# Where the output projections of a cached attention block stand from unit 24 on

## The chip, the cores and the metric

The kernel runs on one core of one Trainium2 chip. The metric is device time in microseconds, the median of five runs. The engines are called as the profile calls them: PE (TensorE matmuls) and PEld (its weight loads), DVE (VectorE), ACT (ScalarE), POOL (GpSimd) and SP (SyncE, which here only issues DMAs).

## The reference

Eight batches of 112 query rows attend to a cache of 512 keys in 32 heads of width 192, with a query projection in front and an output projection behind, all in bf16:

```
B, Sq, D = 8, 112, 640
H, Sk, Dh = 32, 512, 192
q = (x @ wq).reshape(B, Sq, H, Dh).transpose(0, 2, 1, 3)
scores = einsum("bhqd,bhkd->bhqk", q, k_cache) * Dh ** -0.5
p = softmax(scores)
o = einsum("bhqk,bhkd->bhqd", p, v_cache)
out = o.transpose(0, 2, 1, 3).reshape(B, Sq, H * Dh) @ wo
```

## The kernel before

The 32 heads are cut into NG = 8 groups of four. A unit is one batch in one group: NU = 64 units, unit u being group u // 8 and batch u % 8. A unit needs its own K and its own V (four loads of 192 KB each).

**PE's order** is written out in `on_tensor`. Iteration i, from 1 to 63, issues:

1. `do_S(i)` (L954): scores of unit i, 96 small matmuls. The scores fill PSUM banks 0 to 3, which exist once, so `do_S(i)` waits until ACT has taken the exponentials of unit i-1 out (semaphore `aEX`).
2. `do_T(i-2)` (L983): six transposes of the normalised result of unit i-2.
3. `do_pair(i, 0)`: the projection work of slot 0.
4. `do_PV(i-1)` (L972): probabilities times V, 16 matmuls. It waits on `aT` until ACT's copy `tevac(i-2)` (L1069) has taken the transposes of step 2 out, since the two share PSUM banks.
5. `do_pair(i, 1)`: the projection work of slot 1.

Iterations 64 and 65 finish what is left: `do_PV(63)`, two `do_T`, and three projections.

**Projection work** comes in pairs (two PSUM banks, 6 and 7, one for each half h). `("Q", g, c)` is a sixth of the query projection of group g: five steps of two 448-column matmuls. `("O", g, m)` is the output projection of 128 of the 896 output rows for the four heads of group g: six steps of two 320-column matmuls; its result is added into `acc` (or, for the last group, written to `ob`) by DVE in `do_OE` (L1134). A Q pair is taken out by ACT (`evac`, L1036). The first matmul of a step loads the weights (L933), the second keeps them (L858). There are seven O pairs for each group and six Q pairs for each group but the first.

The table `slot[i, j]` says which pair stands in slot j of iteration i. A pair stands there whole (FULL), or its first steps in one slot (FRONT) and the rest in a later one (BACK). `pairs` is the order that results; `bank_free` makes each pair wait until the pair before it in that order has been taken out of the banks.

**DVE's order** in iteration i: two transposes of K (`do_KT`, L1111), the sums of an O pair that ended in slot 0, a third K transpose, reciprocal and scaling of unit i-1 (`do_NM`, L1117 and L1120, after `do_PV(i-1)`), the sums of an O pair that ended in slot 1, a fourth K transpose. From iteration 22 on, the transposes done by the end of iteration i reach the first quarter of unit i+3.

**ACT's order** in iteration i: first exponential of unit i, `tevac(i-2)`, second exponential, Q pair of slot 0, third and fourth exponential, half of the scaling of unit i-1 (`norm`, L1059), Q pair of slot 1. `tevac` of a unit overwrites columns of `oT` that the O pairs of the group before must have read, so it waits on `pO`.

**SP's order** is a list in rounds: in round u, K of unit u, V of unit u-1, then at most one of the five `wq` loads of a later group, then at most one third of the `wo` of a group (two loads of 160 KB). K has three raw buffers, V four, `wo` two; a load waits for its buffer to be free, and everything behind it in the list waits too. The `wo` load of group g waits for the last O pair of group g-2.

Of the kernel before, what the change touches and what calls it, by code (L numbers as in the profile page):

```python
# [666 lines left out]
def build_main(nc, x, k_cache, v_cache, wq, wo, out, flag, regs, hints):  # L667
# [3 lines left out]
    NG = H // 4  # L671
    NU = NG * B
    DC = D // 128
    R = B * SQ
    MT = R // 128
# [9 lines left out]
    FULL, FRONT, BACK = range(3)  # L685
# [12 lines left out]
    slot = {(i, j): None for i in range(NU + 2) for j in range(2)}  # L698

    def put(i, j, pair, part=FULL):  # L700
        assert slot[i, j] is None
        slot[i, j] = (pair, part)

    def halves(i, j, pair):
        put(i, j, pair, FRONT)
        put(i + j, 1 - j, pair, BACK)

    for g in range(NG):
        i0 = 8 * g
        if g > 0 and g < NG - 1:  # L710
            put(i0, 0, ("O", g - 1, 4))
            put(i0, 1, ("Q", g + 1, 0))
            put(i0 + 1, 0, ("O", g - 1, 5))
            halves(i0 + 1, 1, ("Q", g + 1, 1))
            put(i0 + 2, 1, ("O", g - 1, 6))
            put(i0 + 3, 0, ("Q", g + 1, 2))
            halves(i0 + 3, 1, ("Q", g + 1, 3))
            put(i0 + 4, 1, ("O", g, 0))
            put(i0 + 5, 0, ("Q", g + 1, 4))
            halves(i0 + 5, 1, ("Q", g + 1, 5))  # L720
            put(i0 + 6, 1, ("O", g, 1))
            put(i0 + 7, 0, ("O", g, 2))
            put(i0 + 7, 1, ("O", g, 3))
        elif g == 0:
            put(1, 0, ("Q", 1, 0))
            put(1, 1, ("Q", 1, 1))
            put(2, 0, ("Q", 1, 2))
            halves(2, 1, ("Q", 1, 3))
            put(3, 1, ("Q", 1, 4))
            put(4, 0, ("O", 0, 0))  # L730
            halves(4, 1, ("Q", 1, 5))
            put(5, 1, ("O", 0, 1))
            put(6, 0, ("O", 0, 2))
            put(7, 1, ("O", 0, 3))
        else:
            halves(i0, 0, ("O", g - 1, 4))
            halves(i0 + 1, 0, ("O", g - 1, 5))
            put(i0 + 2, 0, ("O", g - 1, 6), FRONT)
            put(i0 + 3, 0, ("O", g - 1, 6), BACK)
            for m in range(4):  # L740
                halves(i0 + 4 + m, 0, ("O", g, m))
            put(i0 + 8, 0, ("O", g, 4))
            put(i0 + 9, 0, ("O", g, 5))
            put(i0 + 9, 1, ("O", g, 6))
    pairs = [slot[i, j][0] for i in range(NU + 2) for j in range(2) if slot[i, j] and slot[i, j][1] != BACK]
    done_at = [slot[i, j][0] for i in range(NU + 2) for j in range(2) if slot[i, j] and slot[i, j][1] != FRONT]
    before = {p: pairs[n - 1] if n else ("Q", 0, 5) for n, p in enumerate(pairs)}
# [3 lines left out]
    assert pairs == done_at and len(pairs) == 6 * (NG - 1) + MT * NG  # L751
    assert [p for p in pairs if p[0] == "Q"] == [("Q", g, c) for g in range(1, NG) for c in range(6)]
    assert [p for p in pairs if p[0] == "O"] == [("O", g, m) for g in range(NG) for m in range(MT)]

    kt_ahead, done = [], 4
    for i in range(NU + 2):
# [4 lines left out]
    with ExitStack() as es:  # L761
# [58 lines left out]
        def W(eng, s, v):  # L820
            if v > 0:
                eng.wait_ge(s, v)

        def bank_of(pair, h):
            return (3, 5)[h] if pair == aside else 6 + h

        def bank_free(eng, pair, h):
            if pair == aside:
                return
            k, g, c = before[pair]  # L830
            if k == "Q":
                W(eng, aQ, q_index[g, c, h] + 1 if g else 11 + h)
            else:
                W(eng, vO, o_index[g, c, h] + 1)
# [4 lines left out]
        def last_unit(m):  # L839
            return -(-128 * (m + 1) // SQ) - 1  # L840
# [6 lines left out]
        def on_tensor(pe):  # L847
# [53 lines left out]
            def do_pair(i, j):  # L901
                if slot[i, j] is None:
                    return
                (k, g, c), part = slot[i, j]
                pair = (k, g, c)
                if k == "Q":
                    if c == 0:
                        W(pe, gW, DC * g)
                    n, width, inc = DC, HQ, pQ
                else:  # L910
                    if part != BACK and 8 * g + last_unit(c) + 1 > min(i - 2 + j, NU - 2):
                        W(pe, aT, 8 * g + last_unit(c) + 1)
                    n, width, inc = 6, HO, pO
                steps = {FULL: range(n), FRONT: range(n // 2), BACK: range(n // 2, n)}[part]
                fill = FILL.get((i, j), 1)
                apart = (i, j) == (NU + 1, 1)
                for q, hs in [(q, [h]) for h in range(2) for q in steps] if apart else [(q, range(2)) for q in steps]:
                    if k == "Q":
                        w = wqs[:, g % 2, q, 128 * c:128 * (c + 1)]
                        rhs = [xT[:, q, HQ * h:HQ * (h + 1)] for h in range(2)]  # L920
                    else:
                        if c == 0 and q % 2 == 0:
                            W(pe, mWO[g % 2][q // 2], 32 * (g // 2 + 1))
                        w = oT[:, q, 128 * c:128 * (c + 1)]
                        rhs = [wos[:, g % 2, q, HL * h:HL + (D - HL) * h] if apart else wos[:, g % 2, q, HO * h:HO * (h + 1)]
                               for h in range(2)]
                    for h in hs:
                        if q == 0:
                            bank_free(pe, pair, h)
                        cuts = fill if q else 1  # L930
                        for f in range(cuts):
                            cs = slice(0, (HL, D - HL)[h]) if apart else slice(width * f // cuts, width * (f + 1) // cuts)
                            mm = (pe.matmul if h == hs[0] and f == 0 else held)(ps[:, bank_of(pair, h), cs], w, rhs[h][:, cs], q == 0,  # L933
                                                                               q == n - 1 and f == cuts - 1)
                        if q == n - 1:
                            mm.then_inc(inc, 1)
# [305 lines left out]
        def on_sync(sp):  # L1242
# [10 lines left out]
            def load_wq(g, dc):  # L1253
                src = wq[128 * dc:128 * (dc + 1), 4 * DH * g:4 * DH * (g + 1)]
                if g == 0:
                    add(wqs[:, 0, dc, :], src, mW0[dc], 16, [])
                else:
                    add(wqr[:, dc, :], src, mWQ[dc], 16 * g, [(gW, DC * (g - 2) + dc + 1)])

            def load_wo(g, k):  # L1260
                r0 = 4 * DH * g + 256 * k
                src = wo[r0:r0 + 256].rearrange("(p e) d -> p e d", e=2)
                for e in range(2):
                    add(wos[:, g % 2, 2 * k + e, :], src[:, e], mWO[g % 2][k], 32 * (g // 2 + 1),
                        [(pO, 2 * MT * (g - 1))])

            def load_k(u):
                g, b = divmod(u, B)
                src = k_cache[b, 4 * g:4 * g + 4].rearrange("a (j s) d -> (a j) (s d)", s=16)
                for h in range(KP[u]):  # L1270
                    cs = slice(16 // KP[u] * DH * h, 16 // KP[u] * DH * (h + 1))
                    add(kr[u % NK][:].rearrange("p s d -> p (s d)")[:, cs], src[:, cs], mK[u % NK], 16 * sum(KP[u % NK:u + 1:NK]),
                        [(vKT, 4 * (u - NK + 1))])

            def load_v(u):
                g, b = divmod(u, B)
                for a in range(4):
                    add(vs[u % NV][:, a, 32:32 + 4 * DH], v_cache[b, 4 * g + a].rearrange("(m t) d -> m (t d)", t=4),
                        mV[u % NV], 64 * (u // NV + 1), [(pPV, u - NV + 1)])
# [16 lines left out]
            for u in range(4, NU + 1):  # L1296
                if u < NU:
                    load_k(u)
                if u - 1 >= 3:
                    load_v(u - 1)  # L1300
                for g in range(2, NG):
                    d = u - max(4, 8 * (g - 1) - 6)
                    if 0 <= d < DC:
                        load_wq(g, d)
                for g in range(1, NG):
                    d = u - (8 * g - 1)
                    if 0 <= d < 3:
                        load_wo(g, d)
            for n, (dst, src, s, count, waits) in enumerate(loads):
# [13 lines left out]
        for part, eng in ((on_tensor, nc.tensor), (on_scalar, nc.scalar), (on_vector, nc.vector), (on_gpsimd, nc.gpsimd), (on_sync, nc.sync)):  # L1323
            part(eng)
# [50 lines left out]
```

## Time and profile before

| | |
|---|---|
| median of five runs | 394.38 us (392.94 to 395.18) |
| the profiled execution's own time | 393.64 us |
| its span on the core | 391.8 us |
| PE busy | 385.5 us (98% of the span) |
| PEld, DVE, ACT, POOL busy | 242.9, 283.4, 250.8, 153.0 us |
| granted TensorE clock | 1.0 |
| moved by DMA | 120.00 MB, mean 306 GB/s |
| chain that ended last | PE 96% |

A time of the profiled execution is compared with its own 393.64 us; the 1.8 us between that and the span lie around the program. A matmul's record is about twice as long as the distance to the next start (the records of neighbours overlap), so distances between starts tell how fast PE goes, and the busy column does not.

### The profile page before, as it was taken

The numbers are of one execution on the slowest core, as the hardware profiler recorded it, in microseconds if no ns is written. First come the engines' busy times: TensorE is split into PE (matmuls) and PEld (weight loads), VectorE is DVE, ScalarE is ACT, GpSimd is POOL, SyncE is SP. The second block draws the span as 40 slices with busy tenths as digits, with TensorE's granted clock in tenths as the row PEclk, the third lists the DMA queues.
The fourth block names the chain that finished last, engine by engine and source line by source line (L and its number), as shares of the span: only waits on it lengthen the run. The fifth ranks groups of instructions, "written<-read, shape, count | busy, mean of one in ns | idle before, by whom it ended". The sixth has DMA issues, their size and how long they took to land.

```text
span 391.8 us, 19832 instructions
## 1 busy us (share of the span) xinstructions
PE 385.5 (98%) x8833; PEld 242.9 (62%) x8286; DVE 283.4 (72%) x506; ACT 250.8 (64%) x550; POOL 153.0 (39%) x352
## 2 busy tenths in 40 slices
PE   8999989999999999999999999999999999999997
PEld 3556665656656665665665665665666665667764
DVE  1665787676786887776787866876768766789935
ACT  3767765766656765657746677557675667657662
POOL 5442543334443354333451354432553332333331
PEclk9999999999999999999999999999999999999999
DMA  8999999999999999999999899989999789999912
GB/s 263 375 371 341 333 321 349 338 303 360 357 360 305 337 301 365 316 310 320 314 337 311 279 310 340 327 286 300 301 341 301 232 298 296 313 318 295 305 53 70
DMA packets 88584, 120.00 MB, mean 306 GB/s; under 512 B 9776, under 2 KB 88496, under 8 KB 88496
## 3 DMA queue, kind: packets, MB, share of 16 engines
q1 hardware_dynamic: 88496, 118.72, 91.4%
q8 instruction: 68, 1.11, 1.2%
q14 instruction: 20, 0.16, 0.1%
HBM read 117.54 MB, written 1.15 MB: 303 GB/s over the span
## 4 chain that ended last, share of the span: by engine, by line
PE 96%; issue 1%; DMA 1%; POOL 1%; DVE 0%; ACT 0%; SPq 0%
PE ps L933 22%; PE ps L972 22%; PE ps L858 21%; PE ps L954 21%; PE ps L983 6%; PE ps L892 2%; DMA xs<-in_x_dram 1%; PE ps L877 1%; PE ps L854 1%; POOL vm L1214 0%; DMA vs<-in_v_cache_dram 0%; PE ps L897 0%; POOL wqs L1207 0%; DVE kt L1111 0%; DVE acc L1131 0%
## 5 line engine op out<-in xcount | busy, mean ns | idle before, releaser
L1111 DVE STREAM_TRANSPOSE kt<-kr 128x384 int32<-128x384 int32 x256 | 195.1, 869 | 11.5 <-DMA kr<-in_k_cache_dram 11.3
L1052 ACT ACTIVATE pT<-ps 128x448 bf16<-128x448 f32 x256 | 130.8, 559 | 84.5 <-PE ps L954 83.6
L954 PEld LDWEIGHTS ps<-qT,kt 32*128 32x128 bf16 x6144 | 77.2, 93 | 30.2 <-issue 22.4
L933 PE MATMUL ps<-wos,oT 128*128 128x320 bf16 (+2 forms) x342 | 93.2, 299 | 0.6 <-issue 0.6
L972 PE MATMUL ps<-vm,pT 128*128 128x193 bf16 x768 | 91.5, 247 | 1.0 <-ACT oT L1069 0.8
L858 PE MATMUL ps<-wos,oT 128*128 128x320 bf16 x330 | 91.2, 299 | 0.0
L954 PE MATMUL ps<-qT,kt 32*128 32x112 bf16 x6144 | 87.8, 208 | 0.6 <-issue 0.4
L1214 POOL COPY vm<-vs 128x1152 int32<-128x1152 int32 x64 | 73.5, 1148 | 32.7 <-issue 25.8
L1231 POOL TENSOR_SCALAR bad<-rinv 112x4 f32<-112x4 f32 x64 | 14.6, 229 | 180.8 <-DVE rinv L1117 180.6
L972 PEld LDWEIGHTS ps<-vm,pT 128*128 128x128 bf16 x768 | 67.9, 97 | 22.1 <-ACT oT L1069 11.6
L933 PE MATMUL ps<-xT,wqs 128*128 128x448 bf16 x210 | 74.0, 352 | 0.3 <-POOL wqs L1207 0.3
L858 PE MATMUL ps<-xT,wqs 128*128 128x448 bf16 x210 | 73.9, 352 | 0.0
L1059 ACT ACTIVATE os<-ps,rinv 112x192 bf16<-112x192 f32 x128 | 48.0, 436 | 27.4 <-DVE rinv L1117 27.4
L972 PE MATMUL ps<-vs,pT 128*128 128x193 bf16 x256 | 62.6, 245 | 0.0
L933 PEld LDWEIGHTS ps<-wos,oT 128*128 128x128 bf16 x342 | 33.2, 97 | 43.7 <-issue 35.8
L1036 ACT ACTIVATE qT<-ps 128x448 bf16<-128x448 f32 x96 | 47.7, 552 | 18.7 <-PE ps L933 13.8
L1134 DVE TENSOR_TENSOR acc<-ps,acc 128x320 f32<-128x320 f32 x84 | 37.3, 485 | 27.6 <-PE ps L933 27.6
L1069 ACT ACTIVATE oT<-ps 128x672 bf16<-128x672 bf16 x64 | 46.4, 725 | 2.1 <-PE ps L983 2.1
L1117 DVE RECIPROCAL rinv<-ps 112x4 f32<-112x4 f32 x64 | 11.1, 173 | 48.0 <-PE ps L972 48.0
L933 PEld LDWEIGHTS ps<-xT,wqs 128*128 128x128 bf16 x210 | 20.4, 97 | 34.5 <-issue 28.9
L1120 DVE TENSOR_TENSOR os<-ps,rinv 112x384 bf16<-112x384 f32 x64 | 35.7, 558 | 7.3 <-DVE rinv L1117 0.5
L1207 POOL COPY wqs<-wqr 128x384 bf16<-128x384 bf16 x70 | 33.3, 510 | 5.0 <-DMA wqr<-in_wq_dram 5.0
(44 smaller groups left out, 154.6 us busy)
## 6 DMA issues: line engine op xcount, KB each, us to landing
kr<-in_k_cache_dram SPq DMA_DIRECT2D x256, 192.0 KB, 4.1
vs<-in_v_cache_dram SPq DMA_DIRECT2D x256, 192.0 KB, 4.0
wos<-in_wo_dram SPq DMA_DIRECT2D x48, 160.0 KB, 4.3
wqr<-in_wq_dram SPq DMA_DIRECT2D x35, 192.0 KB, 5.1
wqs<-in_wq_dram SPq DMA_DIRECT2D x5, 192.0 KB, 4.5
out_dram<-xs SPq DMA_DIRECT2D x6, 160.0 KB, 1.8
xs<-in_x_dram SPq DMA_DIRECT2D x2, 320.0 KB, 3.6
xs<-in_x_dram SPq DMA_DIRECT2D x1, 480.0 KB, 5.7
```

What stands on the lines that cost most here:

```text
L858: return pe.add_instruction(mybir.InstMatmult(name=nc.get_next_instruction_name(), engine=mybir.EngineType.PE, ins=[pe.lower_ap_or_imm(rhs ...
L933: mm = (pe.matmul if h == hs[0] and f == 0 else held)(ps[:, bank_of(pair, h), cs], w, rhs[h][:, cs], q == 0, q == n - 1 and f == cuts - 1)
L954: mm = pe.matmul(ps[:, a, SQ * t:SQ * (t + 1)], kt[u % NT][p, t, c // 2, :, c % 2], qT[g % 2][p, c, SQ * b:SQ * (b + 1)], start=(c == 0), ...
L972: mm = pe.matmul(pv[:, k, e, 0:DH + 1], pT[u % 2][:, a, t, :], src[:, a, v0:v0 + DH + 1], start=(t == 0), stop=(t == 3), skip_group_check= ...
L1036: act.activation(qT[g % 2][:, c, HQ * h:HQ * (h + 1)], ps[:, bank_of_Q0(n) if g == 0 else 6 + h, 0:HQ], ACTF.Copy).then_inc(aQ, 1)
L1052: act.activation(pT[u % 2][:, a, :, 0:SQ], ps[:, a, 0:4 * SQ].rearrange("p (t q) -> p t q", t=4), ACTF.Exp, scale=scale).then_inc(aEX, 1)
L1059: ins = act.activation(os_[u % 2][:, DH * (2 + e):DH * (3 + e)], pv_of(u)[0:SQ, 1, e, 0:DH], ACTF.Copy, scale=rinv[:, u % 4, 2 + e:3 + e])
L1069: act.activation(oT[:, :, SQ * b:SQ * (b + 1)].rearrange("p (k c) q -> p k c q", k=2), src.rearrange("p k (c q) -> p k c q", c=3), ACTF.Co ...
L1111: dve.transpose(dst, src).then_inc(vKT, 1)
L1120: dve.tensor_tensor(os_[u % 2][:, 0:2 * DH].rearrange("p (e d) -> p e d", e=2), pv[0:SQ, 0, :, 0:DH], rinv[:, u % 4, 0:2][:, :, None].broa ...
L1134: ins = dve.tensor_tensor(ob[:, m, cs] if g == NG - 1 else acc[:, m, cs], src, acc[:, m, cs], op=ALU.add)
L1214: gp.tensor_copy(vm[u % NM][:].rearrange("p a (t w) -> p a t w", w=RW)[:, :, :, 0:DH].bitcast(I32), vs[u % NV][:, :, 32:32 + 3 * DH].rearr ...
```

## The change

The slots of units 0 to 23 stay. From unit 24 on the table is filled from a list: the O pairs late by up to one pair in each group of eight units, so that each unit from 24 to 55 holds a whole pair and two or three fifths of a Q pair, and units 56 to 61 hold one and a third or one and two thirds. The fronts that are left are two steps long, of a Q pair (which they were before) and of an O pair (which had three). "f" is FRONT, "b" BACK:

```
unit      before                       after
24        O2.4        Q4.0             O2.4        Q4.0f
25        O2.5        Q4.1f            Q4.0b       O2.5
26        Q4.1b       O2.6             Q4.1        Q4.2f
27        Q4.2        Q4.3f            Q4.2b       O2.6
28        Q4.3b       O3.0             O3.0        Q4.3f
29        Q4.4        Q4.5f            Q4.3b       O3.1
30        Q4.5b       O3.1             Q4.4        Q4.5f
31        O3.2        O3.3             Q4.5b       O3.2
...       (32 to 55 in the same form, in each version)
56        O6.4f       O6.4b            O6.0        O6.1f
57        O6.5f       O6.5b            O6.1b       O6.2
58        O6.6f       -                O6.3        O6.4f
59        O6.6b       -                O6.4b       O6.5
60        O7.0f       O7.0b            O6.6        O7.0f
61        O7.1f       O7.1b            O7.0b       O7.1
62        O7.2f       O7.2b            O7.2        -
63        O7.3f       O7.3b            O7.3        -
64        O7.4        -                O7.4        -
65        O7.5        O7.6             O7.5        O7.6
```

The number of matmuls, of copies and of loads is the same. The round in which `wo` of a group is loaded (`wo_round`) moves, since its buffer comes free later: from 31, 39, 47 and 55 to 32, 41, 50 and 60 for groups 4 to 7. The diff, with the table above standing for the list's details:

```
-        if g > 0 and g < NG - 1:
+        if g in (1, 2):
...
-        else:
-            halves(i0, 0, ("O", g - 1, 4))
...
+    late = [("O", g, m) for g in range(2, NG) for m in range(MT)][4:]
+    stream = []
+    for g in range(3, NG - 1):
+        qs = [("Q", g + 1, c) for c in range(6)]
+        stream += [(late if kind == "O" else qs).pop(0) for kind in "OQOQQOOQOQQO"]
+    stream += late[:-3]
+    counts = [3] * (NU - 26) + [2, 2]
...
+    for i, count in enumerate(counts, 24):
+        for j in range(2):
+            if back:
+                put(i, j, back, BACK)
+                back, count = None, count - 1
+            elif count >= 2:
+                put(i, j, stream.pop(0))
+                count -= 2
+            elif count:
+                back = stream.pop(0)
+                put(i, j, back, FRONT)
+                count -= 1
...
+    wo_round = [0] + [8 * g - 1 for g in range(1, NG)]
+    for g in range(2, NG):
+        wo_round[g] = max(wo_round[g], 5 + max(i for (i, j), it in slot.items() if it and it[0] == ("O", g - 2, MT - 1)))
...
-                steps = {FULL: range(n), FRONT: range(n // 2), BACK: range(n // 2, n)}[part]
+                steps = {FULL: range(n), FRONT: range(2), BACK: range(2, n)}[part]
...
-                    d = u - (8 * g - 1)
+                    d = u - wo_round[g]
```

More of the change, by code (lines that the diff above doesn't have):

```diff
@@ L734, in build_main @@
             put(7, 1, ("O", 0, 3))
-        else:
-            halves(i0, 0, ("O", g - 1, 4))
[L737 to L744, printed above, removed]
+    late = [("O", g, m) for g in range(2, NG) for m in range(MT)][4:]
[5 more added lines that the diff above has]
+    counts = [3] * (NU - 26) + [2, 2]
+    assert sum(counts) == 2 * len(stream)
+    back = None
+    for i, count in enumerate(counts, 24):
[10 more added lines that the diff above has]
+                count -= 1
+        assert count == 0
+    assert not stream and back is None
+    put(NU, 0, late[-3])
+    put(NU + 1, 0, late[-2])
+    put(NU + 1, 1, late[-1])
     pairs = [slot[i, j][0] for i in range(NU + 2) for j in range(2) if slot[i, j] and slot[i, j][1] != BACK]
```

## Prediction

> **What bounds the kernel now.** I read the page first (busy shares, chain), then the stretches, then the waits in the last units, then the timeline there.
>
> ```profile
> PE 385.5 (98%) x8833; PEld 242.9 (62%) x8286; DVE 283.4 (72%) x506; ACT 250.8 (64%) x550; POOL 153.0 (39%) x352
> PE 96%; issue 1%; DMA 1%; POOL 1%; DVE 0%; ACT 0%; SPq 0%
> ```
>
> PE carries the chain. To see where it is held, three stretches: units 1 to 23 roughly, units 24 to 55, units 56 to 62 (time; busy PE, PEld, DVE, ACT, POOL; clock; DMA share; GB/s).
>
> ```profile
> 20.00:157.00 137.00, 134.81 (x3131) 84.55 (x2934) 102.07 (x177) 89.18 (x198) 56.30 (x124) 1.00 1.01 339
> 156.70:345.15 188.45, 188.45 (x4354) 118.49 (x4066) 140.65 (x249) 122.65 (x272) 71.63 (x161) 1.00 0.94 308
> 345.15:377.68 32.53, 32.36 (x899) 22.78 (x864) 27.07 (x50) 22.24 (x49) 11.98 (x27) 1.00 0.82 260
> ```
>
> Busy PE says that only 0.17 us is open in the last stretch. But matmul records overlap (an O matmul has 0.30 us, the next starts 0.135 later), so a hole of under 0.16 us between matmuls is covered by the record before it. What PEld waited for in 345.15 to 381 shows the holes (total, times, longest):
>
> ```profile
> PEld ps L972 <- ACT oT L1069: 3.9, 8, 0.5
> ```
>
> Eight units (56 to 63), each with one wait of 0.49 us of `do_PV`'s first weight load for `tevac`. The timeline of unit 59 (start, length, instruction) shows what it costs PE:
>
> ```profile
> 360.35 0.54 ACT L1052 ACTIVATE pT<-ps 128x448 bf16<-128x448 f32 x1 [0.33 <-PE ps L954]
> 360.56 0.30 PE L933 MATMUL ps<-wos,oT 128*128 128x320 bf16 x1
> ...
> 360.79 0.72 ACT L1069 ACTIVATE oT<-ps 128x672 bf16<-128x672 bf16 x1
> ...
> 361.24 0.30 PE L858 MATMUL ps<-wos,oT 128*128 128x320 bf16 x1
> ...
> 361.57 0.43 PE L972 MATMUL ps<-vm,pT 128*128 128x193 bf16 x3
> ```
>
> Slot 0 holds three O steps: six matmuls from 360.56 to 361.24. The copy ends at 361.51, and PV starts at 361.57: 0.33 after the last O matmul, where 0.135 is the distance without a wait. So PE loses 0.195. With a whole O pair in slot 0 the copy is long over (unit 31: copy from 199.33 to 200.05, last O matmul at 200.60, PV 0.13 later):
>
> ```profile
> 199.33 0.72 ACT L1069 ACTIVATE oT<-ps 128x672 bf16<-128x672 bf16 x1
> ...
> 200.60 0.30 PE L858 MATMUL ps<-wos,oT 128*128 128x320 bf16 x1
> ...
> 200.73 0.42 PE L972 MATMUL ps<-vm,pT 128*128 128x193 bf16 x3
> ```
>
> **A price list for PE.** From starts in the timeline: S 1.29, T 0.31, PV 1.35, the change to the next unit's S 0.10 (every unit has it once): 3.05 us for each unit. An O pair is 12 times 0.135, 1.62; a Q pair 1.89 whole, 1.14 and 0.75 in three and two steps, so that a cut costs under 0.02. Units 24 to 31 in before hold seven O and six Q: 8 x 3.05 + 7 x 1.62 + 6 x 1.89 = 47.08, and their starts (156.70 and 203.81) give 47.11. So PE waits for nothing there. Units 24 to 55: 188.45 measured, 188.3 by the list. Units 56 to 62 hold six O pairs: 7 x 3.05 + 6 x 1.62 = 31.07, measured 32.53. The 1.46 over are seven holes of 0.2; unit 63 has the eighth.
>
> **The change part by part.**
>
> *PE work.* Units 24 to 55 lose four O pairs (24 remain of 28): 32 x 3.05 + 24 x 1.62 + 24 x 1.89 = 181.8. Units 56 to 62 gain them (ten for six): 21.35 + 16.2 = 37.55. Together 219.4, before 221.0. Work only changes places; what goes are the holes: 8 x 0.195 = 1.56. They go since slot 0 of units 56 to 63 now holds 12 or 8 O matmuls. The slot must last 1.01 us (the length of the held block: six matmuls and their hole); 8 matmuls last 1.09 and 12 last 1.63. The cover in units 57, 59 and 61 is thus 0.08 us: if ACT copied later by more than that, each would lose the rest. ACT's part ahead of the copy is one exponential after S in both versions, and no Q pair is left in units 56 to 63, so I take nothing; bounds 0 and 3 x 0.11 (half a hole).
>
> *Banks.* Each pair waits for the one before it to be taken out. New against before are O pairs on either side of PV with only 8 matmuls in the first (57, 59, 61). DVE's two sums last 0.89 and start 0.20 after the last matmul's start; PV lasts 1.35, so they are done about 0.4 before slot 1, if DVE is free. It is: the unit ahead has no sums in its slot 1, so reciprocal, scaling and a transpose (0.2 + 0.75 + 0.77 after PV) end 1.1 into the unit, two transposes more at 2.6, and the first O ends at 2.7. Queued behind such a wait would be PE's whole order. The one unit of before where it happened is 23: sums at 153.24 instead of about 152.95, PV's successor 0.74 late. Bounds: 0 and 3 x 0.74 = 2.2; I take 0.
>
> *ACT.* `tevac` waits for O pairs of the group before to have read `oT`; the tightest is unit 54, copied in iteration 56, whose O5.6 ends with iteration 55: S (1.29) lies between. The last Q pair of a group ends in slot 0 of unit 31 instead of 30; its copies (0.55 each) end about 4.1 into the unit, S of 32 needs them at 5.8. Cost 0; without that cover S would be late by what is missing.
>
> *SP and wo.* The loads of groups 4 to 7 move 1 to 5 rounds back. The wait for the last O of group g-2 is over when the queue arrives: V of the round ahead of it waits for a later PV. The last third for group 7 is issued around unit 59 and lands 4.3 us later (median of wo loads), needed in slot 0 of 61. Cost 0; if it were late, the wait would be PE's. The stores of O7.0 to O7.3 move by under a unit and end before the last one, as now.
>
> *DMA.* Units 24 to 55 get shorter, 188.45 to 181.8 us, with the same 58.0 MB (308 GB/s x 188.45): 319 GB/s wanted. The row for 20 to 157 moved 339 at share 1.01, and 308 has share 0.94, which scales to 328 at full share. So 3 to 6% is left, and K of a unit is transposed 6 to 9 us before its S starts (K of 33: 202.5 and 210.4). I take 0; bounds in the rivals.
>
> [...]
>
> *Tail.* Iterations 64 and 65 hold what they held. PV(63) follows PV(62) directly, 4.58 after S(63) instead of 4.78; the exponentials it needs end 3.86 after. T(62) needs the scaling, 1.14 after PV(62) (381.65 to 382.79 in before); PV(63) covers it with 1.35.
>
> **Sum.** 391.8 - 1.55 = 390.25 span, 392.1 for the profiled execution of 393.64. That execution is 0.74 under the median of 394.38; off the median, 392.8, which is 0.39% less. About 0.3% (1.2 us) is what a measurement of this kernel can tell from no change, so the gain is only just beyond it.
>
> **Rivals.**
> 1. *A bank wait takes the hole's place* (57, 59, 61; `vO`, as in unit 23). 0.74 three times is 2.2: 394.38 - 1.55 + 2.2 = 395.0, no change that can be told; a part of it gives 393.3 to 394.4. For it: two pairs of sums fall in these units (DVE needs 4 x 0.77 + 0.75 + 1.78 = 5.6 of 5.77 us). Against: the units between need 4.7 of 5.2, and K stands far ahead.
> 2. *The holes stay*, because something other than slot 0's length sets PV's start (the change doesn't do what it says): 394.4. Against: unit 31 and all other units with 12 matmuls in slot 0 have no hole.
> 3. *DMA becomes the bound in units 24 to 55* (slower). Place: K or V lands late, DVE's transposes wait, S waits. Before carried 308 GB/s there without a hole, so the worst is a ceiling of just that: 188.45 again instead of 181.8, less about 3 us by which K lands ahead of its transpose (K of 33: 194.7 and 198.3): +3.6, and -1.55 makes +2.1, 396.5. It ends over +1.2 when the rate lasts under about 310 GB/s. Against: 339 at full share.
>
> **Chances.** Forecast (a gain of 1.2 to 1.7): 0.66. Rivals 1 and 2, and measured medians that blur the small gain: 0.26. Rival 3: 0.08. A gain between the cases leaves faster by over 0.3% at 0.68, within 0.24, slower 0.08. The range: down to 1.7 of holes and 1.1 for the spread of the runs (half of 392.94 to 395.18), 391.5; up to rival 1's partial case at 394.6.
>
> **What would show it.** Right: S of unit 56 starts 6.5 us earlier (338.7) and S of 63 near 376.3; units of 5.2 and 5.8 in turn from 56 to 61; no wait of PEld at L992 (L972 now) on ACT `oT` over 0.3 in them. Rival 1 would show as PEld at the pairs' line waiting on DVE, rival 3 as DVE waiting for `kr` after 157 us with a DMA share of 1.0 throughout. The forecast is wrong if any unit from 24 on is over 0.1 above the price list.

## The result, and the profile after

The changed kernel takes 392.87 us in the median (31 runs, 391.19 to 400.32) against 394.7 us for the kernel before on the same chip (52 runs). The ratio is 0.9961, with a 95% interval of 0.9945 to 0.9978: 0.4% faster, a little more than the 0.3% that can be told from nothing. The profiled execution is less plain than that. It took 393.43 us with a span (first to last instruction on the core) of 391.7 us, against 393.64 and 391.8 before.

Busy time and the chain of the changed kernel, from the page, and the row of the queue that carries instructions (packets, MB, share of the DMA engines), which will matter:

```profile
PE 385.7 (98%) x8833; PEld 244.9 (63%) x8286; DVE 283.9 (72%) x506; ACT 249.8 (64%) x550; POOL 153.1 (39%) x352
PE 97%; DMA 1%; DVE 0%; issue 0%; ACT 0%
q8 instruction: 68, 1.11, 1.2%
```

The stretches, cut at the starts of S(24), S(56) and S(63) (time; busy PE, PEld, DVE, ACT, POOL; clock; DMA share; GB/s):

```profile
20.00:157.00 137.00, 135.66 (x3138) 85.04 (x2941) 101.57 (x177) 89.87 (x199) 55.94 (x123) 1.00 1.00 333
156.72:339.40 182.68, 182.52 (x4305) 116.28 (x4041) 137.32 (x241) 121.94 (x272) 72.20 (x161) 1.00 0.96 315
339.40:377.73 38.33, 37.83 (x948) 25.68 (x888) 31.02 (x58) 21.73 (x47) 11.59 (x25) 1.00 0.77 250
```

PE's work moved as the list of slots says: units 24 to 55 take 182.68 us instead of 188.45, units 56 to 62 38.33 instead of 32.53. But the two add up to 221.01, where before had 220.98. By this pair of executions nothing was won.

What PEld waited for from 339.4 us on (total, times, longest):

```profile
PEld ps L953 <- issue: 6.6, 38, 0.2
PEld ps L974 <- issue: 3.6, 9, 0.7
...
PEld ps L992 <- ACT oT L1089: 0.7, 3, 0.2
```

The eight waits of 0.49 for ACT's copy, 3.9 us in all, have become three of 0.2. The timeline of unit 57, where slot 0 has only eight O matmuls (start, length, instruction, idle time before it and its releaser):

```profile
346.22 0.30 PE L953 MATMUL ps<-wos,oT 128*128 128x320 bf16 x1
...
346.45 0.72 ACT L1089 ACTIVATE oT<-ps 128x672 bf16<-128x672 bf16 x1
...
347.17 0.30 PE L878 MATMUL ps<-wos,oT 128*128 128x320 bf16 x1
347.22 0.27 PEld L992 LDWEIGHTS ps<-vm,pT 128*128 128x128 bf16 x3 [0.22 <-ACT oT L1089]
347.31 0.42 PE L992 MATMUL ps<-vm,pT 128*128 128x193 bf16 x3
```

The copy ends at 347.17, as the last O matmul starts, and PV starts 0.14 after that: the distance without a wait. So what the change was to remove has gone. Something else has come, and the second row of the waits names it only as "issue", a wait for nothing that the profile shows, once 0.7 us long. That is S of unit 60:

```profile
361.36 0.47 PE L974 MATMUL ps<-qT,kt 32*128 32x112 bf16 x22
...
362.32 1.11 PE L974 MATMUL ps<-qT,kt 32*128 32x112 bf16 x74 [0.50 <-issue]
362.33 0.95 PEld L974 LDWEIGHTS ps<-qT,kt 32*128 32x128 bf16 x73 [0.66 <-issue]
```

S is a row of 96 matmuls that need nothing from one another. After 22 of them PE stops, and S lasts 2.01 us instead of 1.29. No engine releases it and no semaphore is involved. Unit 60 lasts 5.94 instead of 5.22. Four smaller gaps of the same kind lie in units 25 (0.32), 33 (0.10), 41 (0.18) and 45 (0.14).

**What these gaps are.** In the trace's records of single instructions they all lie at the same count: PE is 193 to 195 instructions past a multiple of 256, weight loads, matmuls and the sequencer's own counted together. PE has 17,178 of them (8,833 matmuls, 8,286 weight loads, 59 others), and the instruction queue above moved 68 packets, one for every 253; 1.11 MB over 68 is 16.3 KB for each. Its packet records give the rest: the packet concerned lands 1.3 to 1.7 us before the gap ends (360.92 for the gap that ends at 362.32; 164.46 for 165.97; 253.32 for 254.62). A packet's transfer starts about when the one before begins to be used (0.9 us before that at the earliest), so PE is hardly more than one packet ahead. Its wait, counted from that moment, is 2.3 us in the median beside the loads of K and V, and 4.0 for the gap of unit 60; a packet lasts 4.7 to 6.0 us from one to the next where there is no gap. From these records I take it that PE waits here for its own instructions. Below such a gap is called a code gap.

The kernel before has them too, and one stood in the prediction under another name. This is its unit 23, the only place behind rival 1's price (a wait of `vO`, 0.74 us):

```profile
154.14 0.24 PE L972 MATMUL ps<-vs,pT 128*128 128x193 bf16 x1
154.96 0.25 PEld L933 LDWEIGHTS ps<-wos,oT 128*128 128x128 bf16 x2 [0.80 <-DVE acc L1134]
154.96 0.31 PE L933 MATMUL ps<-wos,oT 128*128 128x320 bf16 x1 [0.58 <-issue]
```

PEld's row names DVE, since its semaphore is the last one waited for. But the sums that should have held it start at 153.24 and last 0.87: they end at 154.11, before PE stopped. PE's own row has "issue", the count is right for a code gap, and the packet landed at 153.56, 1.40 before its end. From unit 24 on, the profiled execution of before happens to have none.

At most of the 68 packets of an execution PE does not stop; from unit 24 on, none to six of them cost 0.1 to 1.1 us each.

### The profile page after: what moved, and what is told of

Same layout as the page of the kernel before. It is cut to its first block, busy times and chain, and to the rows that moved or that the text cites. A ratio compares the mean times of both kernels' runs of the same rounds, so it can differ in the third digit from the quotient of the medians.

```text
span 391.7 us, 19832 instructions
## 1 busy us (share of the span) xinstructions
PE 385.7 (98%) x8833; PEld 244.9 (63%) x8286; DVE 283.9 (72%) x506; ACT 249.8 (64%) x550; POOL 153.1 (39%) x352
## 3 DMA queue, kind: packets, MB, share of 16 engines
q8 instruction: 68, 1.11, 1.2%
## 4 chain that ended last, share of the span: by engine, by line
PE 97%; DMA 1%; DVE 0%; issue 0%; ACT 0%
PE ps L953 22%; PE ps L992 22%; PE ps L878 22%; PE ps L974 21%; PE ps L1003 6%; PE ps L912 2%; PE ps L897 1%; DMA xs<-in_x_dram 1%; PE ps L874 1%; PE ps L917 0%; DVE kt L1131 0%; DVE acc L1151 0%; ACT oT L1089 0%; ACT pT L1072 0%; DVE xs L1154 0%
```

## The experiments

Eleven runs, in three groups that share their chip and the runs of before. Ratios are of medians against before. One figure recurs: from the start of S(24) to that of S(63), read in each profile, since all that the change does on PE lies there but for the hole of unit 63. The table that closes the section sets it beside the code gaps. A code gap is counted there as what a unit lasts beyond its kind without one.

**The change again.** The unedited kernel, as the yardstick for the others.

> The changed kernel itself, as the yardstick for the others on this chip. Theory: the holes of 0.195 us ahead of PV in units 56 to 63 are gone (1.56 us), and what a single execution gains or loses beside that are holes in PE's stream at every 256th instruction, where PE waits for its own code (the profile after has them at 165.6, 254.4 and 361.6 us, 0.1 to 0.7 us each, always at instruction 193 to 195 of 256). Expected ratio to before 0.996; code holes from unit 24 on between 0.3 and 1.6 us in the profile, in other units than in the profile after. Rival (the holes after are waits for data): they sit in the same units again, away from instruction 193.

392.74 us, ratio 0.9967 (0.9940 to 0.9994). S(24) to S(63) is 220.26 us. There are four code gaps, 0.72 us in all, in units 41, 44, 57 and 59: other places than in the first execution (but for 41), at the same count. So they change from one execution to the next.

**One pair put off.** The kernel before with one edit: O6.3, in before the second pair of unit 55, moves to unit 56, and the pairs behind it follow, so that slot 0 of units 56 to 63 holds one whole pair each.

```
-                put(i0 + 7, 1, ("O", g, 3))
+                if g < NG - 2:
+                    put(i0 + 7, 1, ("O", g, 3))
...
-            halves(i0, 0, ("O", g - 1, 4))
...
-                halves(i0 + 4 + m, 0, ("O", g, m))
+                put(i0 + m, 0, ("O", g - 1, 3 + m))
+                put(i0 + 4 + m, 0, ("O", g, m))
```

> One part alone: units 24 to 54 and the rounds of the wo loads stay as in before; only O6.3 is put off from unit 55 to 56, and with it slot 0 of each of the units 56 to 63 holds one whole O pair. Theory (the gain is the eight holes ahead of PV): all eight go, units 56 to 62 last 4.69 us each, ratio 0.996, the same as the whole change or up to 0.5 us better, since no wo load is moved into the last units. Rival (the gain comes from the even load of units 24 to 55 on DVE, ACT and DMA): ratio 0.999 to 1.000.

394.13 us, ratio 0.9998 (0.9980 to 1.0016): no gain by the time, as the rival had it. The profile has no wait for the copy, and units of 4.67 us in 55 to 62 except 58 (4.78), 59 (5.04) and 61 (5.79). The last is a code gap inside S:

```profile
367.20 0.37 PE L952 MATMUL ps<-qT,kt 32*128 32x112 bf16 x14
...
368.46 1.21 PE L952 MATMUL ps<-qT,kt 32*128 32x112 bf16 x82 [0.89 <-issue]
```

The mechanism did what was expected and the time did not. (This execution is also the slowest of its twelve: behind the last unit, the branch that ends PE's program lasts 3.83 us, where it lasts 0.49 in the profiles of before and of the change.) I formed a second theory here: shorter last units use their code faster, so code takes back what the holes gave. It is tested below.

**Half pairs in the slots again.** The change, with fronts of three steps instead of two, so that slot 0 of units 57, 59 and 61 holds six matmuls.

```
-                steps = {FULL: range(n), FRONT: range(2), BACK: range(2, n)}[part]
+                steps = {FULL: range(n), FRONT: range(n // 2), BACK: range(n // 2, n)}[part]
```

> One line of the change undone: the cut O pairs have three and three steps again, so slot 0 of units 57, 59 and 61 holds six matmuls where it held eight. Theory: three holes of 0.195 us ahead of PV come back there and nowhere else, slot 0 lasts 1.01 us in them instead of 1.09, and the time is 0.5 to 0.6 us over that of the whole change (ratio to before 0.9975). Rival (slot 0's length does not set PV's start): the same time as the whole change, PV right behind slot 0.

392.79 us, ratio 0.9970 (0.9940 to 1.0001): by the time it can't be told from the change; 0.6 us is below what 12 runs resolve. The profile has the three holes back, at the size of before: the waits from 338.4 us on, and unit 57.

```profile
PEld ps L992 <- ACT oT L1089: 1.5, 3, 0.5
```

```profile
345.71 0.72 ACT L1089 ACTIVATE oT<-ps 128x672 bf16<-128x672 bf16 x1
...
346.16 0.30 PE L878 MATMUL ps<-wos,oT 128*128 128x320 bf16 x1
346.48 0.20 PEld L992 LDWEIGHTS ps<-vm,pT 128*128 128x128 bf16 x3 [0.50 <-ACT oT L1089]
346.49 0.43 PE L992 MATMUL ps<-vm,pT 128*128 128x193 bf16 x3
```

0.33 from the last O matmul to PV, 0.195 over the distance without a wait, and pairs of units of 11.18 instead of 10.98. Fronts of two steps thus carry the gain in these three units.

**No wo.** The change without the loads of wo of groups 4 to 7, because the last of these now fall into units 60 to 62, where the longest code gap was seen.

```
-                        if c == 0 and q % 2 == 0:
+                        if c == 0 and q % 2 == 0 and g < 4:
...
-                for g in range(1, NG):
+                for g in range(1, 4):
```

> The changed kernel without the wo loads of groups 4 to 7 (the O pairs of these groups multiply by the weights that groups 2 and 3 left there): 3.9 MB less DMA from 180 us on, nothing else. Theory (PE's code arrives late because its 16 KB packets stand behind data in the DMA rings): from 180 us on the code packets start sooner after the chunk before them (median 2.1 us in the profile after), the hole in unit 60 is gone, code holes after 180 us total under 0.4 us, and the time is 0.3 to 1.2 us under that of the whole change. Rival (code holes do not depend on data traffic): as many of them, and the time of the whole change.

The expectation failed: three code gaps (0.73, 0.23 and 0.39) and a wait of the packets of 1.9 us in the median, hardly shorter than the 2.1 to 2.3 with these loads. They are only 3.9 MB, beside some 58 that units 24 to 55 move. The time is 395.2 us, ratio 1.0046 (1.0029 to 1.0062), but it lies 2.7 us beyond the span in the median (1.6 to 4.4) instead of 1.8, and 4.6 to 4.7 in the four kernels below with fewer loads. The extra stands behind the work: in this profile the last packet of instructions starts 4.0 us after the branch that ends SP's program (394.44 and 390.46), in that of the change 1.3 after (392.90 and 391.61). Why it is late stays open. In six of the twelve runs here (and in four below) under 2.3 us lie beyond the span; these spans are some 3 us longer, so the extra seems to lie inside them. For these kernels I compare the spans of the other runs: here 390.8 us in the median, 390.95 for the change on this chip.

**Less load, three kernels.** Before once more; before, one pair put off, and the change, each without the loads of V of units 24 to 63, to have the holes without code gaps. The place of SP's branch hint moves with the shorter list (26 in the first two, 28 in the change).

```
-    HINT_AT = {"act": 55, "dve": 54, "pool": 40, "sp": 56}
+    HINT_AT = {"act": 55, "dve": 54, "pool": 40, "sp": 26}
...
-                W(gp, mV[u % NV], 64 * (u // NV + 1))
+                W(gp, mV[u % NV], 64 * (min(u // NV, 5) + 1))
...
-                if u - 1 >= 3:
+                if 3 <= u - 1 < 24:
```

> The kernel of before against itself: ratio 1.000, and the width of its interval says what the others can tell. Its profile is a second execution of before. Theory (code holes come and go from execution to execution, and the first profile of before was a lucky one, with under 0.1 us of them from unit 24 on): 0.5 to 1.5 us of holes at instruction 193 to 195 of 256 from unit 24 on, beside the eight holes of 0.195 ahead of PV. Rival (before has no code holes there, only the changed kernel has): again under 0.1 us.

> The kernel before without the V loads of units 24 to 63 (PV goes on with the V that units 20 to 23 left in the buffers): from about 145 us on the DMA queues carry half. Theory (PE's code packets stand behind the data): they start within 0.5 us of the chunk before them, no code hole is left after unit 24, the eight holes ahead of PV stay, and S of unit 24 to S of unit 63 takes 220.9 us in the profile. Rival (code holes have nothing to do with data): 0.5 to 1.5 us of them stay.

> The kernel with O6.3 alone put off, without the V loads of units 24 to 63. Theory: with V it gave its gain back, because its last units (4.67 us) use up a packet of code faster than the next arrives; without V the code is in time and the eight holes ahead of PV are a true gain: S of 24 to S of 63 takes 219.5 us, 1.5 us less than the kernel before without V, ratio of the two 0.996. Rival (holes ahead of PV are not worth their sum, something else takes their place): within 0.4 us of the kernel before without V.

> The changed kernel without the V loads of units 24 to 63. Theory: once the code is in time, the even table has no more to give than the one pair put off: 219.4 us from S of 24 to S of 63, within 0.3 us of the kernel with O6.3 alone put off and without V. Rival (evenness pays by itself, in DVE, ACT or the banks): 0.5 us or more below that kernel.

Before against itself: ratio 1.0004 (0.9977 to 1.0031), with one code gap of 0.64 us in unit 37. It has them from unit 24 on as well, then. The three others have none there. Their packets wait 1.2 us in the median instead of about 2; the theory had expected under 0.5. The start of S(24) and of S(63), from the timelines of before, one pair put off, and the change, all with less V:

```profile
155.51 1.36 PE L954 MATMUL ps<-qT,kt 32*128 32x112 bf16 x96
...
376.51 1.36 PE L954 MATMUL ps<-qT,kt 32*128 32x112 bf16 x96
```

```profile
155.09 1.36 PE L952 MATMUL ps<-qT,kt 32*128 32x112 bf16 x96
...
374.75 1.36 PE L952 MATMUL ps<-qT,kt 32*128 32x112 bf16 x96
```

```profile
156.49 1.36 PE L974 MATMUL ps<-qT,kt 32*128 32x112 bf16 x96
...
376.04 1.36 PE L974 MATMUL ps<-qT,kt 32*128 32x112 bf16 x96
```

221.00, 219.66 and 219.55 us; expected were 220.9, 219.5 and 219.4. Seven holes lie between these starts, 7 x 0.195 = 1.37: one pair put off wins 1.34, the change 1.45. The eighth hole, in unit 63, adds 0.2 (its length is 11.98 and 11.78 in the first two). The 0.11 between these two is unit 58: with one pair put off it lasts 4.78 instead of 4.67, in all four executions of that table, since the transposes wait there for DVE's scaling:

```profile
PEld ps L981 <- DVE os L1118: 0.2, 1, 0.2
```

So the runs show no gain of the even table of units 24 to 55 by itself. In span medians before with less V has 391.15, one pair put off 388.9 and the change 389.6 (leaving out the runs with the extra inside the span). The change is 0.7 behind there. In the two profiles its stretch before unit 24, which neither edits, is 1.4 longer: S(24) starts at 155.09 and at 156.49.

**One pair put off again, and with less load at the end.** To test the second theory: the kernel once more, and without the loads of V of units 53 to 63.

```
-    HINT_AT = {"act": 55, "dve": 54, "pool": 40, "sp": 56}
+    HINT_AT = {"act": 55, "dve": 54, "pool": 40, "sp": 26}
...
-                W(gp, mV[u % NV], 64 * (u // NV + 1))
+                W(gp, mV[u % NV], 64 * (min(u // NV, (52 - u % NV) // NV) + 1))
...
-                if u - 1 >= 3:
+                if 3 <= u - 1 < 53:
```

> The kernel with O6.3 alone put off once more, for a second profile and a narrower interval. Theory (with eight units of 4.67 us in a row a packet of PE's code is used up in 4.65 us, and often comes later than that beside the K and V loads): code holes of 0.7 to 2 us in units 56 to 62, ratio to before between 0.998 and 1.000. Rival (the 1.5 us of code holes in its first profile were an accident, and the kernel is worth the eight holes): under 0.3 us of code holes there and a ratio of 0.996.

> The same kernel without the V loads of units 53 to 63 alone, which are issued from about 311 us on: what is ahead of that stays as it was. Theory (what takes the gain back is the code in the last units, held up by their data): no code hole after 345 us, units 56 to 62 last 4.67 us each, and the span is 1.0 to 1.6 us under that of the kernel with all V loads. Rival: the code holes in units 56 to 62 stay, and the spans are equal within 0.4 us.

The repetition contradicts my theory: 392.68 us, ratio 0.9951 (0.9922 to 0.9981), with a single code gap from unit 24 on (0.47 us in unit 56, more than the 0.3 that the rival allowed). PE's waits in 343.5 to 376.8, against 1.1 us in the first execution of this kernel:

```profile
PE ps L952 <- issue: 0.3, 1, 0.3
```

So code gaps don't always take back what the holes gave. With less V at the end there is no code gap after 345 us, and the packets wait 0.2 us there. The span median is 389.9, against 390.9 for the kernel with all loads on the same chip: 1.0 less, at the edge of the 1.0 to 1.6 expected and about as much as the medians of twelve runs scatter. The time, 394.43 us (0.9997, 0.9969 to 1.0025), has the unexplained part beyond the span.

**More code for the same work.** The change, with the matmuls of O and Q cut in two by columns from unit 24 on: the same products, 542 instructions more (13.6 for each unit, not the 18 of the expectation).

```
-    FILL = {}
+    FILL = {(i, j): 2 for i in range(24, 64) for j in range(2)}
```

> The changed kernel with more code: in units 24 to 63 every projection matmul but those of a pair's first step is issued as two of half the width, about 18 matmuls more for each unit, which carry the same columns. By the distances between starts (1.4 ns over the columns' own time for each matmul) the matmuls themselves cost 40 units x 18 x 1.4 ns = 1.0 us. Theory (a unit's code must arrive within its time): packets of 256 instructions are used up in 5.2 to 5.4 us instead of 5.6, code holes after unit 24 grow from 0.7 to 1.5 us to 2 to 5 us, and the time is 2 to 5 us over that of the changed kernel. Rival (code holes do not depend on how fast code is used): 1.0 us over it.

394.78 us, ratio 1.0008 (0.9982 to 1.0034). The change had 0.9967 on its chip, so the loss is 1.6 us, with 1.5 either way; it lies between the rival's 1.0 and the theory's 2. Units 24 to 55 last 5.46, 5.85 and 5.72 instead of 5.43, 5.81 and 5.69. That and the last units make 1.35 us over all for the matmuls alone (2.5 ns for each of the 542), where the expectation had 1.0. The code gaps come to 2.1 us (in units 25, 26, 31, 35, 45 and 59), against 1.5 and 0.7 in the two profiles of the change. That is at the lower end of what the theory expected, and by one execution it can't be told from chance. So this run leans to the theory and does not settle it.

**The books.** S(24) to S(63) less the code gaps there, us:

```
                                 S(24) to S(63)   code gaps   rest
before                               220.98          0       220.98
before again                         221.64          0.64    221.00
before, less V                       221.00          0       221.00
the change                           221.01          1.46    219.55
the change again                     220.26          0.72    219.54
the change, no wo                    220.93          1.35    219.58
the change, less V                   219.55          0       219.55
one pair put off                     221.14          1.48    219.66
one pair put off again               220.12          0.47    219.65
one pair put off, less V             219.66          0       219.66
one pair put off, less V at the end  220.20          0.55    219.65
half pairs again                     220.82          0.67    220.15
cut                                  223.04          2.1     220.9
```

Every kernel that ran more than once has one rest, within 0.05 us, whatever its code gaps were. By the way a gap is counted, the rest is little more than the sum of the units without one; the rows with no gap (220.98, 221.00, 219.55, 219.66) show the schedule without taking anything out. From before to the change they differ by 1.43: the seven holes, 1.37, and little more. With half pairs in three slots again, 0.60 of it is back, for three holes of 0.195.

## Why the prediction was right

*The holes and the price list.* 8 x 0.195 = 1.56 us was the gain. The rests give 1.43 and unit 63 another 0.2. The list gave 219.4 us for units 24 to 62; the rest is 219.55. In time, the ratio of 0.9961 is 1.5 us, and the repetition 1.2. Spans of both kernels on one chip stand beside the repetition: medians 392.2 us for before (35 runs) and 390.95 for the change (12), means 392.46 and 391.27. So the gain is there, 1.2 to 1.5 us by the figure one takes, with code gaps and the start mixed in. That the sum of 392.8 met the measured 392.87 so closely is in part luck: before was 394.7 in these runs, not the 394.38 it started from.

*The signs.* Units from 56 on last 5.22, 5.76, 5.22, 5.76, 5.94, 5.76 and 4.68 us: 5.2 and 5.8 in turn, but for unit 60. No wait for the copy is over 0.3. S(56) was to start at 338.7 and starts at 339.40, S(63) at 377.73 instead of 376.3. The difference is code gaps, 0.74 and 0.72 us; without them the two starts are 338.66 and 376.27. By the last sign, no unit over 0.1 above the list, the forecast would have been called wrong: five units were, one of them (33) barely. That sign supposed that nothing but the schedule could lengthen a unit.

*What was costed at nothing.* The banks: no wait of a pair for DVE's sums shows in 57, 59 or 61, or anywhere from unit 24 on, and rival 1 did not come. Its price was wrong all the same, read from a code gap. ACT and the tail: as costed. DMA: units 24 to 55 moved 315 GB/s at a share of 0.96 without a wait for K or V, so rival 3 did not come, and the row with 339 was the right one to go by; the stretch to 157 us has 333 this time, again with loads of 192 KB.

*SP and wo.* The loads of group 7 came in time for their matmuls. But now they lie in the last units, beside K and V (the stretch of the change around unit 60, columns as above):

```profile
359.00:366.00 7.00, 6.50 (x145) 4.04 (x131) 5.29 (x11) 3.67 (x9) 1.80 (x4) 1.00 1.01 327
```

Before moved 295 GB/s in the same time at a share of 0.98. The instruction packets from 345 to 380 us wait 2.28 us in the median, against 0.37. That is a cost the prediction did not name. But the kernel with one pair put off, whose wo loads stay where before has them, has 1.4 there in both its profiles, and the kernel without these loads has 1.7 and code gaps all the same. So how much the move of wo adds is not shown.

*The missing term.* PE's own instructions, 0 to 1.5 us from unit 24 on, in before and in the change alike: about the size of the gain. The prediction said "PE waits for nothing there" of before, which held for the one execution it had. Over executions the term falls on both kernels, and so the sum of differences came out about right. Whether it falls equally is open: two profiles of before have 0 and 0.64 us, two of the change 1.46 and 0.72. A prediction that leaves out a term as large as its gain is right with some luck.

*What part of the change does it.* One O pair put off does: its rest is within 0.11 us of the change's. Its two runs gave 0.9998 and 0.9951; its span medians, each against before on the same chip, are 392.45 to 392.2 and 390.9 to 392.6. No run shows a version that is clearly better than the change.

## What to carry to other kernels

Price the steps of the engine that bounds the kernel from starts in the timeline, and add them up: 1.5 us of holes in 8 units stood out so clearly, while busy time showed 0.17. Before a wait is given to an engine, look whether that engine's instruction really ended with it; a wait on "issue" in a row of like instructions, at a fixed count of instructions (193 to 195 past a multiple of 256), was a code gap here. Where the gain is about 1 us, compare the same stretch in several executions and take out what changes between them.

## What the runs showed of the hardware

In the profiles of before and of the change PE's instructions come in packets of 16.3 KB on the instruction queue (68 packets, 1.11 MB). From unit 24 on, one is started about when the packet before it begins to be used (from 0.9 us before to 4.0 us after), and where PE stops, it goes on 1.3 to 1.7 us after the packet has landed. Beside the loads of units 24 to 62 (308 and 315 GB/s in units 24 to 55) it waits 1.8 us (before) and 2.3 us (the change) in the median to start and moves in about 1 us. That fits into the 4.1 to 6.5 us that a packet lasts in these two profiles, but with little room: a start that came late made PE stop for 0.1 us (unit 33 of the change) to 1.1 us (unit 61 with one pair put off). With half the traffic (162 GB/s, before with less V) the wait fell to 1.2 us, and in the three kernels without V no packet came late from unit 24 on.
